# Reordering GpSimd's queue and the weight steps in the attention rounds of a decay attention, SwiGLU and maxout kernel

## The chip, the cores and the metric

One core of a Trainium2 chip runs the whole program. The metric is the device time of one execution in microseconds (us), read as the median of several. The engines are TensorE (PE; PEld is its weight load), VectorE (DVE), ScalarE (ACT), GpSimd (POOL) and SyncE (SP, which here only issues DMAs).

## The reference

A causal linear attention with a decay per head (2 x 8 heads, 768 tokens, 64 per head, blocks of 64), then an RMS norm and a SwiGLU layer (1536 tokens, 512 to 1536 to 512), then the maximum of three products and an output product (512 to 768 to 512).

```python
intra = einsum('bhic,bhjc->bhij', qb, kb) * Dmask       # Dmask = lam ** (i - j), i >= j
intra = einsum('bhij,bhjd->bhid', intra, vb)
inter = einsum('bhid,bhde->bhie', qb * lam_pow, kv_state)
out = intra + inter
kv_state = lam_block * kv_state + einsum('bhsd,bhse->bhde', kb * rev_pow, vb)
...
xn = x / sqrt(mean(x * x) + 1e-06) * rms_g
g = xn @ w_gate
x = (g * sigmoid(g) * (xn @ w_val)) @ w_out
...
h = maximum(maximum(x @ w1, x @ w2), x @ w3)
out = h @ w_out2
```

## The kernel before

Products in fp32 are made of three matmuls of halves: each operand is split into a high half (`xh`, `wh`, `hh`, a cast on ACT) and a low half (`xl`, `wl`, `hl`, the remainder, mostly on POOL).

**Attention** goes over 12 chunks of 128 tokens in software-pipelined rounds 0, 1, 2 and so on. A round is a list of steps, one letter each (`named`, L429), each of them a stage of another chunk:

- M (L379, chunk s-2): the mix of state and scores on PE into `px`, then ACT writes the squares `sq` and the scaled `x`; from chunk 4 on DVE sums the squares (`ss`, L392).
- C (L313, chunk s-1): scores and new states on PE into `sc`, from `kT`, `qT`, the scaled keys `kd` and `vn`.
- a, b (L328, chunk s-1): DVE masks the two halves into `A` (L331); a also advances the state `S` (L349). V (L353, chunk s-1) advances it once more.
- T (L288, chunk s): loads of chunk s+2 on SP, transposes of k and q on PE into `pk`, `pq`, copies `kT`, `qT` on ACT (L299, L301), `qs` on DVE (L304), and the keys scaled on POOL (`kd`, L285) for this chunk and the next, so in effect for chunk s+1.
- U (L396, chunk s-2): sum over features on PE (`pm`), `ms` on DVE (L403), and the token scale `ri`, a power, on POOL (L405).
- N (L408, chunk s-3): `pb` on PE spreads `ri` over the partitions (L414), DVE multiplies `x` by it (L416), ACT makes `xh` (L418). R (L421, chunk s-3): the low half `xl` (L427), on POOL for the first eight chunks.

All engines execute in the order in which the program issues. In rounds 0 to 6 that is M C a N b R T U V. These seven rounds run as a prologue; later rounds are mixed into the first stage, a few steps at each `gap()` (L439).

**Weights** come as 512 KB loads (L157) into three raw buffers and are turned into halves in units. `make_unit` (L242) moves three units on: it finishes the oldest (`wh` on ACT, `wl` on POOL, L167 and L170), does the three weight steps of the next on DVE (L196, L199, L202) with an addition on POOL behind them (L204), and begins a third with two ACT operations (L238, L239). In the prologue it is called four times, after steps counted by hand (L971), and seven loads are placed in the same way (L973).

**First stage**: for each block of 512 tokens and each hidden slice, a gate product `pg` and a value product `pv` (L604), activation, split, and an output product (L617). Its first product needs `xh` and `xl` of chunks 0 to 3, so N(3) and R(3) of round 6. The rest of the program (maxout and the remaining slices, L874) isn't touched.

```python
named = dict(M=(2, mixed), N=(3, normed), C=(1, scores), a=(1, masked(0)), R=(3, rest),
             b=(1, masked(1)), U=(2, summed), V=(1, advance), T=(0, lambda c: (loads_to(c + 2), turn(c))))
attn_q = [(s_, named[ch][1], s_ - named[ch][0]) for s_ in range(NCH + 3)
          for ch in ("MCaNbRTUV" if s_ <= CPNB + 2 else "MNCRaUbVT") if 0 <= s_ - named[ch][0] < NCH]
```

Of the kernel before, what the change touches and what calls it, by code (L numbers as in the profile page):

```python
# [9 lines left out]
F32 = mybir.dt.float32  # L10
F32R = mybir.dt.float32r
AF = mybir.ActivationFunctionType
ALU = mybir.AluOpType
# [5 lines left out]
P = 128  # L19
# [7 lines left out]
def tile_decay_attention_swiglu_maxout(  # L27
# [16 lines left out]
    nc = tc.nc  # L44
    B, H, S, D = q.shape
    NT, DM = out.shape
    NP = H // 2
# [5 lines left out]
    C = P // 2  # L53
# [3 lines left out]
    CPB = S // P  # L57
    NCH = NT // P
    CPNB = NB // P
# [7 lines left out]
    att = att_ctx.enter_context(tc.tile_pool(name="att", bufs=2))  # L67
# [3 lines left out]
    def bank(name):  # L71
        return psum.tile([P, 512], F32, tag="bank", name=name)
# [9 lines left out]
    Tm = attc.tile([P, H, C], F32, name="Tm")  # L82
# [3 lines left out]
    qkv = {}  # L86
    nxt_load = [0]

    def load(c, n):
        t = ld.tile([P, H, D], F32, tag="kqv"[n], name="kqv"[n] + "n", bufs=4 if n == 2 else 3)  # L90
        b, s = divmod(c, CPB)
        nc.sync.dma_start(out=t, in_=(k, q, v)[n][b, :, s * P:(s + 1) * P, :].rearrange("h p d -> p h d"))
        qkv.setdefault(c, {})[n] = t

    def loads_to(c):
        while nxt_load[0] <= min(c, NCH):
            n = nxt_load[0]
            if n:
                load(n - 1, 2)
            if n < NCH:  # L100
                load(n, 0)
                load(n, 1)
            nxt_load[0] += 1
# [7 lines left out]
    def crosswise(t, src):  # L111
        return [(t[:, 0::2], src[:, 0::2])] + [(t[HC[m], 1::2], src[HC[1 - m], 1::2]) for m in range(2)]
# [37 lines left out]
    pos = {"load": 0, "made": 0, "raw": 0, "step": 0, "gap": 0, "quiet": False, "lag": 3, "narrow": True, "seam": False}  # L150

    def load_to(n):
        while pos["load"] < min(n, len(raw_list)):
            nm, f = raw_list[pos["load"]]
            t = wp.tile([P, KD, 2 * P], I32, tag="raw", name="wraw", bufs=3)
            for to, src in crosswise(t, source[nm](f)) if nm in "gv" else [(t, source[nm](f))]:
                nc.sync.dma_start(out=to, in_=src)  # L157
            raws[nm, f] = t
            pos["load"] += 1
# [82 lines left out]
    def make_unit():  # L242

        if stage2:
            finish_unit(*stage2.pop(0))
        if stage1:
            unit = stage1.pop(0)
            for n in range(3):
                words_of_unit(n, *unit)
            stage2.append(unit[:3])  # L250
        begin_unit()
# [27 lines left out]
    keys = {}  # L279

    def decayed_keys(c):
        if c not in keys:
            keys[c] = kd = att.tile([P, H, D], F32, tag="kd", name="kd", bufs=3)
            r = slice(0, P if c % CPB != CPB - 1 else C)
            nc.gpsimd.tensor_tensor(out=kd[r], in0=qkv[c][0][r], in1=Tm[r, :, C - 1:C].to_broadcast([r.stop, H, D]),  # L285
                                    op=ALU.mult)

    def turn(c):  # L288
        kn, qn, vn = qkv[c][0], qkv[c][1], qkv[c][2]
        pk = bank("pk")  # L290
        pq = bank("pq")
        pkv = pk.rearrange("p (a t) -> p a t", t=P)
        pqv = pq.rearrange("p (a t) -> p a t", t=P)
        for a in range(NP):
            nc.tensor.transpose(pkv[:, a, :], kn[:, 2 * a:2 * a + 2, :].rearrange("p h d -> p (h d)"), ident)
        for a in range(NP):
            nc.tensor.transpose(pqv[:, a, :], qn[:, 2 * a:2 * a + 2, :].rearrange("p h d -> p (h d)"), ident)
        kT = att.tile([P, NP, P], F32, tag="kT", name="kT")
        nc.scalar.copy(out=kT, in_=pkv)  # L299
        qT = att.tile([P, NP, P], F32, tag="qT", name="qT")  # L300
        nc.scalar.copy(out=qT, in_=pqv)  # L301
        qs = att.tile([P, NP, 2, C], F32, tag="qs", name="qs")
        h0 = 0 if c % CPB else 1
        nc.vector.tensor_tensor(  # L304
            out=qs[:, :, h0:], in0=pqv.rearrange("p a (h i) -> p a h i", h=2)[:, :, h0:],
            in1=lami.rearrange("p a (h i) -> p a h i", h=1).to_broadcast([P, NP, 2 - h0, C]), op=ALU.mult)
        for n in range(c, min(c + 2, NCH)):
            decayed_keys(n)
        kd = keys.pop(c)
        A = att.tile([P, H, C], F32, tag="A", name="A")  # L310
        st[c] = dict(kT=kT, qT=qT, qs=qs, kd=kd, vn=vn, A=A)
# [16 lines left out]
    def masked(hf):  # L328
        def piece(c):
            d = st[c]  # L330
            nc.vector.tensor_tensor(  # L331
                out=d["A"].rearrange("p (a t) i -> p t a i", t=2)[:, hf],
                in0=d["sc"][hf][:, :HF].rearrange("p (a i) -> p a i", i=C),
                in1=Tm.rearrange("p (a t) i -> p t a i", t=2)[:, hf], op=ALU.mult)
            if hf == 0:
                d["S0"] = last_state[0]
                d["S1"] = next_state(c, 0, d["S0"])
        return piece
# [40 lines left out]
    def mixed(c):  # L379
        for part in range(2):  # L380
            half_mixed(c, part)
        px = st[c]["px"]
        sq = att.tile([P, NP, P], F32, tag="sq", name="sq", bufs=1)
        x = att.tile([P, NP, P], F32, tag="x", name="x")
        for n in range(2):
            nc.scalar.activation(out=sq[:, 2 * n:2 * n + 2, :], in_=px[n][:, :2, :], func=AF.Square)
        for a in range(NP):
            nc.scalar.activation(out=x[:, a, :], in_=px[a // 2][:, a % 2, :], func=AF.Copy, scale=g_sb[:, a:a + 1])
        ss = sq
        if c >= CPNB:  # L390
            ss = att.tile([P, 1, P], F32, tag="ss", name="ss", bufs=1)
            nc.vector.tensor_reduce(out=ss[:, 0, :], in_=sq.rearrange("p a t -> p t a"),  # L392
                                    axis=mybir.AxisListType.X, op=ALU.add)
        st[c] = dict(x=x, ss=ss)
# [26 lines left out]
    def rest(c):  # L421
# [5 lines left out]
        eng.tensor_tensor(out=bl[:, :, ts], in0=x, in1=bh[:, :, ts].bitcast(F32), op=ALU.subtract)  # L427

    named = dict(M=(2, mixed), N=(3, normed), C=(1, scores), a=(1, masked(0)), R=(3, rest),  # L429
                 b=(1, masked(1)), U=(2, summed), V=(1, advance), T=(0, lambda c: (loads_to(c + 2), turn(c))))  # L430
    attn_q = [(s_, named[ch][1], s_ - named[ch][0]) for s_ in range(NCH + 3)
              for ch in ("MCaNbRTUV" if s_ <= CPNB + 2 else "MNCRaUbVT") if 0 <= s_ - named[ch][0] < NCH]
    gaps = [0, 0]

    def attn_step():
        _, fn, c = attn_q.pop(0)
        fn(c)
# [505 lines left out]
    with tc.manual_schedule():  # L943
        nc.scalar.dma_start(out=lam8, in_=lam.rearrange("(o h) -> o h", o=1).to_broadcast([P, H]))
        loads_to(0)
        for to, src in crosswise(g_sb, rms_g.rearrange("(a p) -> p a", p=P)):
            nc.scalar.dma_start(out=to, in_=src)
        make_identity(nc, ident)
        nc.vector.memset(ones, 1.0)
        nc.vector.memset(zeros, 0.0)  # L950
        nc.scalar.activation(out=mhalf, in_=zeros[:, 0:1], func=AF.Silu)
        nc.vector.memset(mhalf, -0.5)
        warm = bank("warm")
        for i in range(9):
            nc.tensor.matmul(out=warm[:, 0:P], lhsT=zeros, rhs=zeros, start=True, stop=True)
        nc.vector.tensor_tensor(out=diag, in0=ident[:, :C], in1=ident[:, C:], op=ALU.add)
        for h in range(H):
            nc.vector.tensor_tensor_scan(
                out=Tm[:, h, :], data0=lam8[:, h:h + 1].to_broadcast([P, C]), data1=diag,
                initial=0.0, op0=ALU.mult, op1=ALU.add)  # L960
        for hf in range(2):
            nc.vector.tensor_copy(out=lamh[64 * hf:64 * hf + 64, :],
                                  in_=lam8.rearrange("p (a t) -> p t a", t=2)[64 * hf:64 * hf + 64, hf, :])
        for a in range(NP):
            nc.vector.tensor_tensor_scan(
                out=lami[:, a, :], data0=lamh[:, a:a + 1].to_broadcast([P, C]), data1=zeros[:, :C],
                initial=1.0, op0=ALU.mult, op1=ALU.add)
        loads_to(1)
        for i in range(sum(1 for p in attn_q if p[0] <= CPNB + 2)):
            attn_step()  # L970
            if i in (17, 26, 35, 46):  # L971
                make_unit()
            load_to(pos["load"] + (4, 8, 14, 31, 40, 48, 48).count(i))  # L973
        finish = first_stage()
        pos["step"] = len(steps)
        second_stage(finish)
# [31 lines left out]
```

## Time and profile before

| | us |
|---|---|
| median of 3 runs | 553.53 (552.24 to 554.17) |
| profiled execution | 553.25 |
| its span, first to last instruction | 551.5 |
| PE busy in the span | 531.9 (96%) |
| DVE, ACT, POOL busy | 377.5, 278.7, 316.9 |

The span is what the profile sees; 1.75 us of the execution lie around it. PE is the busy engine: from the middle of the first stage on it hardly pauses, and the first 55 us, with the attention rounds, hold most of its idle time. A row of the order of time gives start, duration, engine, line, operation, output and inputs, and in brackets the idle time before it and what released it. Starts within one engine can lie closer than the durations, since operations overlap at their ends.

### The profile page before, as it was taken

What the parts mean: (1) busy time and instruction counts of PE and PEld (TensorE: products, weight loads), DVE (VectorE), ACT (ScalarE), POOL (GpSimd) and SP (SyncE); (2) the same over time, 40 slices, a digit from 0 to 9 for tenths busy, and PEclk for the clock granted to TensorE, in tenths of its full rate; (3) what the DMA queues carried; (4) which work ended last, traced back from release to release, by engine and by line L of the source; (5) the groups of instructions that cost most, each with busy time, mean ns of one, the idle gap of its engine ahead of it and who ended that gap; (6) DMA issues with size and microseconds to landing.
All of it is one profiled execution on the core that took longest, in us unless ns stands there. A gap on an engine that the chain in (4) does not pass through costs nothing.

```text
span 551.5 us, 9707 instructions
## 1 busy us (share of the span) xinstructions
PE 531.9 (96%) x3716; PEld 440.9 (80%) x3716; DVE 377.5 (68%) x664; ACT 278.7 (51%) x541; POOL 316.9 (57%) x251
## 2 busy tenths in 40 slices
PE   7778998999999999999999999999999999999997
PEld 7776876888888888888888888888888888888885
DVE  6567988545797567566786686877777577684464
ACT  3565665354475675346346436556466655551120
POOL 2366988312799558155545737986396544962050
PEclk9876999999999999999999999999999999999999
DMA  8984566200203214121221312120123322200014
GB/s 188 228 209 121 143 160 161 64 2 1 77 0 116 76 38 116 38 71 45 78 68 47 114 40 77 40 76 13 64 78 96 97 76 76 80 35 1 0 52 178
DMA packets 65454, 44.67 MB, mean 81 GB/s; under 512 B 40064, under 2 KB 61568, under 8 KB 65408
## 3 DMA queue, kind: packets, MB, share of 16 engines
q1 hardware_dynamic: 64704, 44.05, 28.0%
q8 instruction: 29, 0.48, 0.3%
q14 instruction: 17, 0.14, 0.1%
q10 hardware_dynamic: 704, 0.01, 0.1%
HBM read 40.90 MB, written 3.15 MB: 80 GB/s over the span
## 4 chain that ended last, share of the span: by engine, by line
PE 82%; DVE 4%; POOL 4%; ACT 2%; issue 2%; DMA 1%; SPq 0%; POOLq 0%; ACTq 0%; DVEq 0%
PE p L675 34%; PE r L675 8%; PE acc L467 6%; PE acc L469 6%; PE acc L468 6%; PE q L675 4%; PE acc L858 3%; PE acc L857 3%; PE acc L859 3%; PE pv L467 2%; POOL W L204 2%; PE pv L469 1%; PE pv L468 1%; PE pg L467 1%; PE pg L469 1%
## 5 line engine op out<-in xcount | busy, mean ns | idle before, releaser
L204 POOL TENSOR_TENSOR W<-W,wraw 128x512 int32<-128x512 int32 x60 | 81.6, 1361 | 84.7 <-DVE W L202 71.6
L170 POOL TENSOR_TENSOR wl<-W,wh 128x512 fp32r<-128x512 f32 x77 | 105.3, 1368 | 42.3 <-ACT wh L167 42.1
L167 ACT CAST wh<-W 128x512 fp32r<-128x512 f32 x77 | 47.8, 620 | 87.5 <-POOL W L204 87.0
L481 POOL TENSOR_TENSOR hl<-sg,hh 128x512 fp32r<-128x512 f32 x36 | 48.7, 1352 | 25.2 <-ACT hh L480 25.2
L675 PE MATMUL p<-xh,wh 128*128 128x512 f32 x148 | 57.6, 389 | 0.0
L675 PE MATMUL p<-xl,wh 128*128 128x512 f32 x148 | 57.6, 389 | 0.0
L675 PE MATMUL p<-xh,wl 128*128 128x512 f32 x148 | 57.6, 389 | 0.0
L467 PE MATMUL acc<-hh,wh 128*128 128x512 f32 x144 | 56.6, 393 | 0.0
L468 PE MATMUL acc<-hl,wh 128*128 128x512 f32 x144 | 56.1, 389 | 0.0
L469 PE MATMUL acc<-hh,wl 128*128 128x512 f32 x144 | 56.0, 389 | 0.0
L830 DVE TENSOR_TENSOR acc_sb<-acc,acc_sb 128x512 f32<-128x512 f32 x46 | 31.8, 691 | 21.7 <-PE acc L469 20.6
L238 ACT ACTIVATE W<-wraw 128x512 f32<-128x512 f32 x60 | 40.1, 669 | 4.8 <-DMA wraw<-in_moe_w_dram 2.8
L239 ACT ACTIVATE wraw<-wraw 128x512 int32<-128x512 uint32 x60 | 39.9, 664 | 0.0
L480 ACT CAST hh<-sg 128x512 fp32r<-128x512 f32 x36 | 22.3, 619 | 33.5 <-DVE sg L614 24.9
L730 ACT COPY c<-p 128x512 f32<-128x512 f32 x34 | 19.9, 586 | 38.0 <-PE p L675 37.9
L481 POOL TENSOR_TENSOR hl<-m,hh 128x512 fp32r<-128x512 f32 x18 | 24.1, 1346 | 23.0 <-ACT hh L480 23.0
L675 PE MATMUL p<-yh,wh 128*128 128x512 f32 x90 | 35.0, 389 | 0.0
L675 PE MATMUL p<-yl,wh 128*128 128x512 f32 x90 | 35.0, 389 | 0.0
L675 PE MATMUL p<-yh,wl 128*128 128x512 f32 x90 | 35.0, 389 | 0.0
L196 DVE TENSOR_SCALAR mid<-W 128x512 f32<-128x512 f32 x46 | 31.5, 685 | 3.4 <-ACT W L238 3.4
L675 PEld LDWEIGHTS p<-xl,wh 128*128 128x128 f32 x148 | 27.8, 188 | 5.8
L675 PEld LDWEIGHTS p<-xh,wh 128*128 128x128 f32 x148 | 27.8, 188 | 5.8
(175 smaller groups left out, 1369.6 us busy)
## 6 DMA issues: line engine op xcount, KB each, us to landing
wraw<-in_moe_w_out_dram SPq DMA_DIRECT2D x18, 512.0 KB, 3.4
wraw<-in_moe_w_dram SPq DMA_DIRECT2D x18, 512.0 KB, 3.5
kn<-in_k_dram SPq DMA_DIRECT2D x12, 256.0 KB, 4.5
qn<-in_q_dram SPq DMA_DIRECT2D x12, 256.0 KB, 4.7
vn<-in_v_dram SPq DMA_DIRECT2D x12, 256.0 KB, 4.5
wraw<-in_moe_w_gate_dram SPq DMA_DIRECT2D x12, 256.0 KB, 3.0
wraw<-in_moe_w_gate_dram SPq DMA_DIRECT2D x24, 128.0 KB, 3.4
wraw<-in_moe_w_val_dram SPq DMA_DIRECT2D x12, 256.0 KB, 3.0
```

The source lines that it names most:

```text
L167: nc.scalar.copy(out=wh, in_=W.bitcast(F32))
L170: nc.gpsimd.tensor_tensor(out=wl, in0=W.bitcast(F32), in1=wh.bitcast(F32), op=ALU.subtract)
L196: nc.vector.tensor_scalar(out=mid[key].bitcast(F32), in0=W.bitcast(F32), scalar1=LEAST, scalar2=MOST, op0=ALU.max, op1=ALU.min)
L204: nc.gpsimd.tensor_tensor(out=W, in0=W, in1=lo, op=ALU.add)
L238: nc.scalar.activation(out=W.bitcast(F32), in_=hi.bitcast(F32), func=AF.Abs)
L239: nc.scalar.activation(out=lo, in_=lo.bitcast(U32), func=AF.Copy, scale=2.0 ** -29)
L467: nc.tensor.matmul(out=out, lhsT=wh, rhs=xh_, start=first, stop=False)
L468: nc.tensor.matmul(out=out, lhsT=wh, rhs=xl_, start=False, stop=False)
L469: nc.tensor.matmul(out=out, lhsT=wl, rhs=xh_, start=False, stop=last)
L481: nc.gpsimd.tensor_tensor(out=dst_l, in0=src, in1=dst_h.bitcast(F32), op=ALU.subtract)
L675: nc.tensor.matmul(out=ps, lhsT=w[:, ks], rhs=r[:, o + k, :], start=first and k == 0 and n == 0, stop=k == 1 and n == 2, skip_group_check= ...
L830: nc.vector.tensor_tensor(out=ps if kept else y, in0=ps, in1=y, op=ALU.add)
```

## The change

- POOL: `kd` of the next chunk becomes a step of its own, K, at the end of the round, and R stands behind U. So in rounds 0 to 6 POOL gets ri, xl, kd where it got xl, kd, ri. Rounds are now M C a N b T U R V K, and later M N C a U b V T K R.
- The four `make_unit` calls of the prologue stand at the ends of rounds 3, 4, 5 and 6; before, they stood behind b in rounds 3, 4 and 5 and behind T in round 6.
- The seven weight loads of the prologue stand at the ends of rounds 2 to 6 (1, 1, 1, 2, 2).
- `x` has three buffers instead of two.

```diff
@@ decayed_keys
     def decayed_keys(c):
-        if c not in keys:
-            keys[c] = kd = att.tile([P, H, D], F32, tag="kd", name="kd", bufs=3)
...
+        keys[c] = kd = att.tile([P, H, D], F32, tag="kd", name="kd", bufs=3)
...
@@ turn
-        for n in range(c, min(c + 2, NCH)):
-            decayed_keys(n)
+        if c == 0:
+            decayed_keys(0)
@@ mixed
-        x = att.tile([P, NP, P], F32, tag="x", name="x")
+        x = att.tile([P, NP, P], F32, tag="x", name="x", bufs=3)
@@ named, attn_q
-                 b=(1, masked(1)), U=(2, summed), V=(1, advance), T=(0, lambda c: (loads_to(c + 2), turn(c))))
+                 b=(1, masked(1)), U=(2, summed), V=(1, advance), T=(0, lambda c: (loads_to(c + 2), turn(c))), K=(-1, decayed_keys))
...
-              for ch in ("MCaNbRTUV" if s_ <= CPNB + 2 else "MNCRaUbVT") if 0 <= s_ - named[ch][0] < NCH]
+              for ch in ("MCaNbTURVK" if s_ <= CPNB + 2 else "MNCaUbVTKR") if (ch == "K") <= s_ - named[ch][0] < NCH]
@@ the prologue
-        for i in range(sum(1 for p in attn_q if p[0] <= CPNB + 2)):
-            attn_step()
-            if i in (17, 26, 35, 46):
+        for s_ in range(CPNB + 3):
+            while attn_q[0][0] == s_:
+                attn_step()
+            load_to(pos["load"] + (0, 0, 1, 1, 1, 2, 2)[s_])
+            if s_ > 2:
                 make_unit()
-            load_to(pos["load"] + (4, 8, 14, 31, 40, 48, 48).count(i))
```

DVE in rounds 4 and 5, before: from the state update of round 4's V over round 5 to that of round 5. W is the weight unit, sc0 and sc1 the scores of one chunk.

```order
L349 SCALAR_TENSOR_TENSOR S_615<-S_563,lami_81,sc1_529 128x64 x4
L331 TENSOR_TENSOR A_605<-sc0_667,Tm_80 128x4x64
L349 SCALAR_TENSOR_TENSOR S_702<-S_615,lami_81,sc0_667 128x64 x4
L416 TENSOR_TENSOR x_521<-x_521,pb_707 128x512
L331 TENSOR_TENSOR A_605<-sc1_668,Tm_80 128x4x64
L196 TENSOR_SCALAR W_577<-W_577 128x512
L199 TENSOR_SCALAR W_577<-W_577 128x512
L202 SCALAR_TENSOR_TENSOR W_577<-wraw_306,W_577 128x512
L304 TENSOR_TENSOR qs_744<-pq_731,lami_81 128x512
L403 TENSOR_SCALAR ms_754<-pm_749 128x1
L349 SCALAR_TENSOR_TENSOR S_758<-S_702,lami_81,sc1_668 128x64 x4
```

The same place of the changed kernel, from round 5's first mask to round 6's.

```order
L330 TENSOR_TENSOR A_593<-sc0_663,Tm_80 128x4x64
L348 SCALAR_TENSOR_TENSOR S_698<-S_604,lami_81,sc0_663 128x64 x4
L415 TENSOR_TENSOR x_519<-x_519,pb_703 128x512
L330 TENSOR_TENSOR A_593<-sc1_664,Tm_80 128x4x64
L303 TENSOR_TENSOR qs_728<-pq_715,lami_81 128x512
L402 TENSOR_SCALAR ms_736<-pm_731 128x1
L348 SCALAR_TENSOR_TENSOR S_741<-S_698,lami_81,sc1_664 128x64 x4
L196 TENSOR_SCALAR W_617<-W_617 128x512
L199 TENSOR_SCALAR W_617<-W_617 128x512
L202 SCALAR_TENSOR_TENSOR W_617<-wraw_476,W_617 128x512
L391 TENSOR_REDUCE ss_810<-sq_802 128x128
L330 TENSOR_TENSOR A_730<-sc0_812,Tm_80 128x4x64
```

The three weight steps moved from between the second mask and `qs` to behind the round's last state update and ahead of the next round's `ss` and first mask.

POOL in rounds 5 and 6, before; xl_436 from x_521 is chunk 2's low half, from x_656 chunk 3's.

```order
L170 TENSOR_TENSOR wl_713<-W_442,wh_712 128x512
L204 TENSOR_TENSOR W_577<-W_577,wraw_306 128x512
L427 TENSOR_TENSOR xl_436<-x_521,xh_435 128x4x128
L285 TENSOR_TENSOR kd_746<-kn_583,Tm_80 128x512
L405 TENSOR_TENSOR ri_756<-ms_754,mhalf_79 128x1
L427 TENSOR_TENSOR xl_436<-x_656,xh_435 128x4x128
L285 TENSOR_TENSOR kd_872<-kn_726,Tm_80 128x512
L170 TENSOR_TENSOR wl_876<-W_577,wh_875 128x512
L204 TENSOR_TENSOR W_720<-W_720,wraw_427 128x512
L405 TENSOR_TENSOR ri_890<-ms_888,mhalf_79 128x1
```

And in the changed kernel.

```order
L404 TENSOR_TENSOR ri_738<-ms_736,mhalf_79 128x1
L426 TENSOR_TENSOR xl_430<-x_519,xh_429 128x4x128
L284 TENSOR_TENSOR kd_746<-kn_573,Tm_80 128x512
L170 TENSOR_TENSOR wl_757<-W_480,wh_756 128x512
L204 TENSOR_TENSOR W_617<-W_617,wraw_476 128x512
L404 TENSOR_TENSOR ri_876<-ms_874,mhalf_79 128x1
L426 TENSOR_TENSOR xl_430<-x_656,xh_429 128x4x128
L284 TENSOR_TENSOR kd_879<-kn_710,Tm_80 128x512
L170 TENSOR_TENSOR wl_888<-W_617,wh_887 128x512
L204 TENSOR_TENSOR W_764<-W_764,wraw_611 128x512
```

Each `ri` moved ahead of the same round's `xl` and `kd`, and the weight unit's `wl` and `W` from the round's middle to its end. In round 6, chunk 3's `xl` now stands behind `ri` of chunk 4.

## Rows read from the trace of the kernel before

**Rows 1.** Busy time by stretch: first pieces of the first stage, then the rest of the interleaving.

```profile
43.50:54.00 10.50, 8.79 (x86) 5.98 (x90) 8.05 (x11) 6.04 (x15) 8.55 (x7) 0.51 0.45 115
...
55.00:120.00 65.00, 60.72 (x844) 49.14 (x841) 48.55 (x103) 36.76 (x83) 43.23 (x35) 1.00 0.44 113
```

**Rows 2.** Groups by line, 20 to 58 us: busy, mean ns, idle before and its releasers.

```profile
L414 PE MATMUL pb<-ident,ri 128*128 128x128 f32 x8 | 2.6, 422 | 4.3 <-POOL ri L405 3.5 <-DMA wraw<-in_moe_w_val_dram 0.8
...
L405 POOL TENSOR_TENSOR ri<-ms,mhalf 128x1 f32<-128x1 f32 x4 | 2.4, 592 | 0.0
...
L403 DVE TENSOR_SCALAR ms<-pm 128x1 f32<-128x1 f32 x5 | 0.7, 148 | 0.0
```

**Rows 3.** Order of time on ACT, round 3: start us, us, what.

```profile
20.36 0.62 ACT L418 CAST xh<-x 128x512 fp32r<-128x512 f32 x1 [2.41 <-DVE x L416]
...
20.89 0.67 ACT L238 ACTIVATE W<-wraw 128x512 f32<-128x512 f32 x1
...
22.03 0.56 ACT L299 COPY kT<-pk 128x512 f32<-128x512 f32 x1
```

**Rows 4.** Order of time on DVE, rounds 3 and 4.

```profile
18.49 0.42 DVE L331 TENSOR_TENSOR A<-sc,Tm 128x256 f32<-128x256 f32 x1 [2.25 <-PE sc L324]
...
19.60 0.68 DVE L416 TENSOR_TENSOR x<-x,pb 128x512 f32<-128x512 f32 x1
...
23.11 0.69 DVE L304 TENSOR_TENSOR qs<-pq,lami 128x512 f32<-128x512 f32 x1 [2.50 <-ACT qT L301]
...
23.78 0.85 DVE L349 SCALAR_TENSOR_TENSOR S<-S,lami,sc 128x64 f32<-128x64 f32 x4
...
25.11 0.42 DVE L331 TENSOR_TENSOR A<-sc,Tm 128x256 f32<-128x256 f32 x1 [0.48 <-PE sc L324]
```

**Rows 5.** Order of time on DVE, round 4: first and third weight step, POOL idle.

```profile
27.36 0.42 DVE L196 TENSOR_SCALAR W<-W 128x512 f32<-128x512 f32 x1
...
28.27 0.69 DVE L202 SCALAR_TENSOR_TENSOR W<-wraw,W 128x512 int32<-128x512 int32 x1
```

**Rows 6.** Order of time on DVE and POOL, round 6 and after: weight steps beside POOL.

```profile
44.47 0.42 DVE L304 TENSOR_TENSOR qs<-pq,lami 128x256 f32<-128x256 f32 x1 [1.32 <-ACT qT L301]
...
44.77 1.06 POOL L285 TENSOR_TENSOR kd<-kn,Tm 128x512 f32<-128x512 f32 x1
...
44.81 1.31 DVE L196 TENSOR_SCALAR W<-W 128x512 f32<-128x512 f32 x1
...
46.15 1.39 DVE L199 TENSOR_SCALAR W<-W 128x512 int32<-128x512 int32 x1
...
47.57 0.69 DVE L202 SCALAR_TENSOR_TENSOR W<-wraw,W 128x512 int32<-128x512 int32 x1
...
54.68 1.74 DVE L202 SCALAR_TENSOR_TENSOR W<-wraw,W 128x512 int32<-128x512 int32 x1
```

**Rows 7.** Order of time on DVE and POOL, round 6: ss(4), x(3), xl(3).

```profile
40.06 1.05 DVE L392 TENSOR_REDUCE ss<-sq 128x128 f32<-128x512 f32 x1 [0.79 <-ACT sq L386]
...
42.13 0.68 DVE L416 TENSOR_TENSOR x<-x,pb 128x512 f32<-128x512 f32 x1
...
43.54 1.27 POOL L427 TENSOR_TENSOR xl<-x,xh 128x512 fp32r<-128x512 f32 x1 [2.10 <-ACT xh L418]
```

**Rows 8.** Order of time on PE, first projection: the second matmul, and pb(4).

```profile
44.86 0.79 PE L468 MATMUL pg<-xl,wh 128*128 128x512 f32 x1 [0.70 <-POOL xl L427]
...
50.55 0.80 PE L414 MATMUL pb<-ident,ri 128*128 128x128 f32 x2 [0.89 <-POOL ri L405]
```

**Rows 9.** SP's queue in order of time, and time to landing of the gate loads.

```profile
18.41 0.59 SPq L92 DMA_DIRECT2D vn<-in_v_dram  x1
...
19.73 2.15 SPq L92 DMA_DIRECT2D qn<-in_q_dram  x1
...
wraw<-in_moe_w_gate_dram SPq DMA_DIRECT2D x3, 256.0 KB, 5.3
```

**Rows 10.** Order of time on PE, 94 us.

```profile
94.15 0.47 PE L467 MATMUL pv<-xh,wh 128*128 128x512 f32 x1 [1.50 <-DVE x L416]
```

More of the change, by code (lines that the diff above doesn't have):

```diff
@@ L281, in decayed_keys @@
     def decayed_keys(c):
-        if c not in keys:
-            keys[c] = kd = att.tile([P, H, D], F32, tag="kd", name="kd", bufs=3)
-            r = slice(0, P if c % CPB != CPB - 1 else C)
-            nc.gpsimd.tensor_tensor(out=kd[r], in0=qkv[c][0][r], in1=Tm[r, :, C - 1:C].to_broadcast([r.stop, H, D]),
-                                    op=ALU.mult)
+        keys[c] = kd = att.tile([P, H, D], F32, tag="kd", name="kd", bufs=3)
+        r = slice(0, P if c % CPB != CPB - 1 else C)
+        nc.gpsimd.tensor_tensor(out=kd[r], in0=qkv[c][0][r], in1=Tm[r, :, C - 1:C].to_broadcast([r.stop, H, D]),
+                                op=ALU.mult)
     def turn(c):
```

## The prediction

> **What bounds the kernel now.** I read the views in this order. The busy table by stretch: from 55 to 120 us TensorE (PE) works 60.72 of 65.00 us at full clock, and in 43.5 to 54.0, the first gated projections, it runs at a granted clock of 0.51 and is busy 8.79 of 10.50 us [rows 1]. So what a change to the attention rounds can move lies before about 55 us, plus the 4.28 us that PE idles in 55 to 120. Then the groups by line in 20 to 58 us: PE stood 4.3 us in front of `pb`, mostly waiting for GpSimd's power `ri` [rows 2]. That is the wait at which the new queue order aims. Then the order of time on VectorE (DVE), ScalarE (ACT), GpSimd (POOL) and PE in rounds 3 to 7, from which the sum is made. Rounds are counted from 0; x(3) means chunk 3's `x`. The profiled execution took 553.25 us, the median of the runs shown is 553.53; the sum goes by the former and 0.3% of it, about what a measurement can tell from no change, is 1.66 us.
>
> **Step 1, round 3: a gain of 1.6 us.** Before, ACT runs xh(0) at 20.36, then the first weight unit's two operations from 20.89, and only at 22.03 the copies kT(3) and qT(3) [rows 3]. Now the copies come first, so kT(3) starts at 20.89, 1.14 us earlier, and qs(3) on DVE at 21.97 instead of 23.11 [rows 4]. Its `ms` and the state update follow and end 24.63 - 23.11 = 1.52 us after qs starts, so at 23.49. PE's sc(3), which waited for qT(3), starts at about 22.0 and is done before that, so A(3) starts at 23.5 instead of 25.11 [rows 4]: 1.6 us ahead.
>
> **Step 2, a DVE round without weight steps: 5.0 us.** From A to x 19.60 - 18.49 = 1.11 [rows 4]. From x to qs: x lasts 0.68 with 0.08 until ACT's xh at 20.36; 0.53 until ACT's next operation (20.36 to 20.89), which is now kT; and 1.08 from kT's start at 22.03 over qT to qs at 23.11 [rows 3, 4]: 2.37. From qs to the end of S 1.52. Sum 5.0 us. pb no longer holds it up, because `ri` now stands first.
>
> **Step 3, the weight steps on DVE: 3.45 and 4.5 us, and they lie in the chain.** Alone, the three (L196, L199, L202) take from 27.36 to 28.96, 1.6 us [rows 5]. Beside a working POOL they wait: L196 beside `kd` 1.31 us instead of 0.42, L199 1.39, and the three end at 48.26 after a start at 44.81, so 3.45 us; L202 met by a POOL operation took 1.74 instead of 0.69 [rows 5, 6]. Before, rounds 4 and 5 have them after the second A and ahead of qs, where DVE waits for qT anyway and POOL stood empty. Now they come after S, while POOL goes through ri, xl and kd, all released by the `ms` just ahead, so L196 meets xl and L199 meets kd, and nothing can keep them apart. In round 4 POOL has nothing more until L202 is done: 3.45. In round 5 wl waits there as well: 3.45 + 1.74 - 0.69 = 4.5. DVE's next A is queued behind them. ACT's part of the weight steps (unit after qT) is hidden by that same DVE stretch.
>
> The Trainium skill's page SBUF — State Buffer, section Who interferes with whom, says that VectorE and GpSimd share one port pair, that whichever starts first keeps it for its whole instruction, and that `tensor_scalar` in its two-port mode and operations with two SBUF inputs fall under it. This speaks against the change, and the rows agree (1.31 against 0.42 us). By the rule the sum is the one below, +2.6; were there no such lock, it would be -2.2.
>
> **The chain.** A(3) 23.5; A(4) = 23.5 + 5.0 + 3.45 = 31.95; the sum ss(4) = 31.95 + 5.0 + 4.5 = 41.45 against 40.06; x(3), 2.07 behind it, 43.5 against 42.13 [rows 7]: **+1.4 us**, the lead of step 1 lost and more.
>
> **Step 4, the low half xl(3): +2.1 us.** The first projection's second matmul (L468, at 44.86) reads xl(3) [rows 8]. Before, xl(3) starts 43.54 - 42.13 = 1.41 after x(3) [rows 7]. Now POOL takes ri(4) ahead of it, and that needs qs(6) and ms(4): 2.37 + 0.42 + 0.15 + 0.59 = 3.53 [rows 2, 6]. That is 2.1 more, straight on PE's path, since PE is in order and nothing else stands ahead of L468.
>
> **Step 5, pb(4): -0.9 us.** PE waited 0.89 for ri(4) between two pieces of that projection [rows 8]; ri(4) now comes before xl(3), so this is gone. The earlier pb waits of rows 2 are gone too, but DVE, not PE, sets the rounds then, so they count nothing; that is what becomes of the stall the change removes.
>
> **Edits at nothing.** The third buffer of x takes away ACT's wait for an older xl; x(c) is used a round later, so a round's slack covers it. kd moves behind xl and ri and is read a round later; without that cover it would cost its 1.06 us [rows 6]. On SP's queue seven weight loads move behind attention loads, the first behind three more (v, k, q). Those three took 3.5 us of the queue, from 18.41 to 21.88, and a gate load lands 5.3 us after its issue by the median [rows 9]; a whole round lies between a load's place and its use by ACT, so I expect no wait, or little; bounds 0 and +1.0, off DVE's chain, taken as 0. What follows in 55 to 120 is reshuffled, ten steps to a round instead of nine; the longest single PE wait there is 1.50, at 94.15 [rows 10], so bounds of -1.5 and +1.5, taken as 0 for want of a row that favours a sign. Clock: up to 54.0 it was half [rows 1]. Half over the same work again: 0. The piece from pb(4) at 50.55 to 54.0, 3.45 us [rows 8], at full rate instead: -1.7; half rate for as much work more: +1.7. I take 0, what the nearest rows show for a PE that has just been waiting.
>
> **Sum:** +1.4 + 2.1 - 0.9 = +2.6. Forecast 553.25 + 2.6 = **555.8 us**, 2.3 above the median.
>
> **Rivals.**
> *Faster: the weight steps don't collide or are covered.* Then they cost 1.6 each, 7.95 - 3.2 = 4.75 less, and the sum is -2.2: 551.1 us. For it: alone they do take 1.6 [rows 5]. Against: POOL's three operations are released by the instruction right ahead. It decides once the two groups together cost under 5.3 us.
> *Same: the clock stays up.* With the waits for ri and qT gone PE idles less, and the half-rate stretch may end earlier. From L468 at 44.86 to 54.0 it is 9.1 us with 0.9 of wait, so full rate throughout would save at most 4.1, and a clock that rises in its middle 2.1: 553.7. Against: by my chain PE waits for A(4) up to some 3 us in round 6 and again for xl(3), so it idles there more than before. The Trainium skill's TensorE: Matmul & The Clock Gate (Part 1: The HAM clock gate) says that the clock has two states, falls after idling and rises with sustained work; the trace shows both levels (0.51 and 1.00), and by that rule a prologue with fewer waits would give this rival's time.
> *Same, later absorbed.* PE is not full in 55 to 120; a start 2.6 us late could be won back from its 4.28 us of waits: 553.3. Against: those waits hang on banks and DVE, not on the clock of the start.
>
> **How the numbers follow.** Forecast case 0.47 (slower). The two rivals of no change together 0.28. The uncovered gain 0.25. Low end: 551.1 less 1.7 for the clock, 549.4. High end: 555.8 plus 1.5 for a new later wait and 1.7 for the clock, 559.0. The likeliest case alone: from the edge of no change, 555.2, to 559.0. Faster 0.25, same 0.28, slower 0.47.
>
> **What would show it.** Right: L196 and L199 of rounds 4 and 5 at 1.2 us or more, directly after S; PE free of waits for ri; the gap from xh(3) to xl(3) over 2 us; L468 2 to 4 us later than 44.86. Wrong: L196 at 0.42 there, or L468 at or before 44.86; then the first rival holds. If L468 is late and the end is not, the clock row or the waits in 55 to 120 tell which of the other two it was.

## The result, and the profile after

The changed kernel takes 561.25 us (median of 4 runs, 560.44 to 562.23) against 553.85 for the kernel before in the same comparison: ratio 1.0136, 95% interval 1.0103 to 1.0169, or 7.4 us slower. The sign of the forecast was right and the size was not: +2.6 was expected, and the range ended at 559.0. The profiled execution took 560.44, its span 558.6.

Busy time by stretch of the changed kernel, for the two stretches of [rows 1] (columns: stretch, its length, then busy us of PE, PEld, DVE, ACT, POOL, then granted clock, DMA share, GB/s):

```profile
43.50:54.00 10.50, 6.95 (x76) 5.07 (x77) 7.53 (x10) 5.21 (x11) 7.48 (x7) 0.54 0.58 148
55.00:120.00 65.00, 57.35 (x801) 43.98 (x795) 49.02 (x97) 33.57 (x74) 42.52 (x35) 0.97 0.44 115
```

PE does 1.84 us less in the first stretch than in [rows 1], and 3.37 us less in the second. So more is lost behind 55 us than ahead of it.

**The prologue went as worked out.** VectorE in the changed kernel: the weight steps of round 4, then round 6 with ss(4), x(3) and ms(4):

```profile
28.29 1.48 DVE L196 TENSOR_SCALAR W<-W 128x512 f32<-128x512 f32 x1
29.81 1.16 DVE L199 TENSOR_SCALAR W<-W 128x512 int32<-128x512 int32 x1
...
40.80 1.02 DVE L391 TENSOR_REDUCE ss<-sq 128x128 f32<-128x512 f32 x1
...
42.84 0.67 DVE L415 TENSOR_TENSOR x<-x,pb 128x512 f32<-128x512 f32 x1
...
45.56 0.15 DVE L402 TENSOR_SCALAR ms<-pm 128x1 f32<-128x1 f32 x1
```

L196 takes 1.48 us here, where it took 0.42 alone [rows 5], and L199 behind it 1.16. ss(4) at 40.80 and x(3) at 42.84 are 0.7 later than in [rows 7]. These are single executions: four other runs below (e3, e6, e8, e10) have the same first rounds, and their x(3) starts between 42.56 and 44.42.

**GpSimd's queue at the end of the prologue.** First the changed kernel, then the kernel before. L170 is the low part of a weight unit:

```profile
40.95 1.28 POOL L204 TENSOR_TENSOR W<-W,wraw 128x512 int32<-128x512 int32 x1 [0.63 <-DVE W L202]
45.79 0.75 POOL L404 TENSOR_TENSOR ri<-ms,mhalf 128x1 f32<-128x1 f32 x1 [3.56 <-DMA wraw<-in_moe_w_val_dram]
46.42 1.26 POOL L426 TENSOR_TENSOR xl<-x,xh 128x512 fp32r<-128x512 f32 x1
47.64 1.51 POOL L284 TENSOR_TENSOR kd<-kn,Tm 128x512 f32<-128x512 f32 x1
49.11 1.45 POOL L170 TENSOR_TENSOR wl<-W,wh 128x512 fp32r<-128x512 f32 x1
...
101.72 1.29 POOL L170 TENSOR_TENSOR wl<-W,wh 128x512 fp32r<-128x512 f32 x1 [0.73 <-ACT wh L167]
```

```profile
45.78 1.47 POOL L170 TENSOR_TENSOR wl<-W,wh 128x512 fp32r<-128x512 f32 x1
...
95.51 1.29 POOL L170 TENSOR_TENSOR wl<-W,wh 128x512 fp32r<-128x512 f32 x1 [0.73 <-ACT wh L167]
```

GpSimd stands idle for 3.56 us in front of ri(4). The profile names a DMA, but ri starts right behind `ms` on DVE (45.56), which is its input; this is a case where the engine named isn't the one waited for. In the queue behind ri stand not only xl(3), 2.88 us later than in [rows 7], but also kd and the weight unit's low part, the second one of the program: 49.11 instead of 45.78, **3.3 us late**. The last rows of the two fences are the twelfth low part: **6.2 us late**. So the chain of weight units, which goes through DVE, POOL, ACT and POOL again, starts late and ends later still, but not by a steady growth: the fourth low part is 1.5 us late (57.29 for 55.83), the ninth 0.9 (83.63 for 82.76), and the tenth, in the third hidden slice, 5.5 (92.42 for 86.96).

**TensorE: the late start is nearly won back, and then lost.** Order of time on PE in the changed kernel:

```profile
44.27 0.80 PE L466 MATMUL pg<-xh,wh 128*128 128x512 f32 x1 [2.01 <-ACT xh L417]
...
47.74 0.79 PE L467 MATMUL pg<-xl,wh 128*128 128x512 f32 x1 [2.67 <-POOL xl L426]
...
55.72 0.50 PE L466 MATMUL pv<-xh,wh 128*128 128x512 f32 x1
```

The second matmul is 2.88 us later than in [rows 8], the first value product only 0.76 (54.96 before). Of the 2.12 us won back, 0.89 is the wait for ri(4) of [rows 8], which is gone; most of the rest is the clock. The stretch from 53 to 54 us, before and then after:

```profile
53.00:54.00 1.00, 1.00 (x11) 0.35 (x13) 1.00 (x3) 0.28 (x2) 0.22 (x1) 0.52 0.06 25
```

```profile
53.00:54.00 1.00, 1.00 (x6) 0.87 (x5) 0.00 (x0) 1.00 (x4) 1.00 (x2) 0.88 0.79 254
```

By these means (0.52 and 0.88, between levels of 0.50 and 1.00) full rate came at about 53.96 before and 53.24 after, 0.7 us earlier, though TensorE was further behind in its work. Behind that, TensorE's waits in the changed kernel from 43 to 125 us (total, times, longest) are of a kind that the kernel before hardly has there:

```profile
PE pg L467 <- POOL xl L426: 4.0, 2, 2.7
PE pg L468 <- POOL wl L170: 2.7, 2, 2.0
PE pv L468 <- POOL wl L170: 2.2, 2, 1.2
PE pg L466 <- ACT xh L417: 2.0, 1, 2.0
```

The low parts of weights, 4.9 us in four waits, are new; before, the longest single wait from 55 us on was the 1.50 for x of [rows 10].

**Why the chain loses more on its way.** ScalarE's order in the first hidden slice, changed kernel and then before (`sg` is the silu, `hh` the high half of the hidden block):

```profile
59.46 0.59 ACT L298 COPY kT<-pk 128x512 f32<-128x512 f32 x1 [1.11 <-PE pk L294]
60.42 0.62 ACT L612 ACTIVATE sg<-pg 128x512 f32<-128x512 f32 x1
61.90 0.62 ACT L479 CAST hh<-sg 128x512 fp32r<-128x512 f32 x1 [0.85 <-DVE sg L613]
```

```profile
56.04 0.58 ACT L613 ACTIVATE sg<-pg 128x512 f32<-128x512 f32 x1
59.06 0.62 ACT L480 CAST hh<-sg 128x512 fp32r<-128x512 f32 x1 [2.43 <-DVE sg L614]
...
61.24 0.57 ACT L299 COPY kT<-pk 128x512 f32<-128x512 f32 x1
```

With R gone from its place near the front of a round and ten steps dealt out instead of nine, T falls into an earlier gap, ahead of the silu. Either alone leaves it behind the silu: ten steps with R early in e6, nine steps with R late in e15. The copies wait for transposes, the silu behind them waits too, and through hh it holds GpSimd's low half hl. In the third slice it costs most. ACT, POOL and PE of the changed kernel:

```profile
87.21 0.58 ACT L298 COPY kT<-pk 128x512 f32<-128x512 f32 x1 [2.52 <-PE pk L294]
88.55 0.59 ACT L300 COPY qT<-pq 128x512 f32<-128x512 f32 x1 [0.75 <-PE pq L296]
89.03 0.60 ACT L612 ACTIVATE sg<-pg 128x512 f32<-128x512 f32 x1
```

```profile
91.19 1.28 POOL L480 TENSOR_TENSOR hl<-sg,hh 128x512 fp32r<-128x512 f32 x1 [2.91 <-ACT hh L479]
92.42 1.74 POOL L170 TENSOR_TENSOR wl<-W,wh 128x512 fp32r<-128x512 f32 x1
```

```profile
94.21 0.50 PE L468 MATMUL pg<-xh,wl 128*128 128x512 f32 x1 [0.64 <-POOL wl L170]
```

GpSimd waits 2.91 us for hh with the next weight unit queued behind it. Before, hl ran without a wait:

```profile
85.54 1.46 POOL L481 TENSOR_TENSOR hl<-sg,hh 128x512 fp32r<-128x512 f32 x1
```

From the third gate product to the fourth it is 19.5 us now (73.33 to 92.86), 14.0 before (73.94 to 87.90).

### The profile page after: what moved, and what is told of

Same layout as the page of the kernel before. It is cut to its first block, busy times and chain, and to the rows that moved or that the text cites. A ratio compares the mean times of both kernels' runs of the same rounds, so it can differ in the third digit from the quotient of the medians.

```text
span 558.6 us, 9707 instructions
## 1 busy us (share of the span) xinstructions
PE 534.4 (96%) x3716; PEld 439.5 (79%) x3716; DVE 385.1 (69%) x664; ACT 279.0 (50%) x541; POOL 317.4 (57%) x251
## 4 chain that ended last, share of the span: by engine, by line
PE 81%; POOL 7%; DVE 4%; DMA 3%; issue 2%; ACT 1%; SPq 1%; POOLq 0%; ACTq 0%; DVEq 0%
PE p L674 33%; PE r L674 8%; PE acc L466 5%; PE acc L468 5%; PE acc L467 5%; PE q L674 4%; PE acc L857 3%; PE acc L858 3%; PE acc L856 3%; POOL W L204 2%; POOL wl L170 2%; PE pv L468 2%; PE pv L466 2%; PE pv L467 1%; PE pg L467 1%
## 5 line engine op out<-in xcount | busy, mean ns | idle before, releaser
L170 POOL TENSOR_TENSOR wl<-W,wh 128x512 fp32r<-128x512 f32 x77 | 105.5, 1370 | 40.8 <-ACT wh L167 40.8
L468 PE MATMUL acc<-hh,wl 128*128 128x512 f32 x144 | 56.1, 389 | 0.0
L196 DVE TENSOR_SCALAR mid<-W 128x512 f32<-128x512 f32 x46 | 31.5, 685 | 3.4 <-ACT W L238 3.4
L199 DVE TENSOR_SCALAR mid<-mid 128x512 int32<-128x512 int32 x46 | 31.9, 694 | 0.7
```

Of the source, the lines that this page charges most:

```text
L170: nc.gpsimd.tensor_tensor(out=wl, in0=W.bitcast(F32), in1=wh.bitcast(F32), op=ALU.subtract)
L199: nc.vector.tensor_scalar(out=mid[key], in0=mid[key], scalar1=0x07FFFFFF, scalar2=3, op0=ALU.bitwise_and, op1=ALU.logical_shift_left)
L468: nc.tensor.matmul(out=out, lhsT=wl, rhs=xh_, start=False, stop=last)
```

## The experiments

Theory: the loss comes from GpSimd's weight chain, late at the start behind ri and xl(3) and later behind the hl that T's new place holds up. Rivals: the collisions on DVE, the places of the loads, the ten steps, the late place of the low halves. Each run was compared with its own runs of the kernel before (medians 552.5 to 553.9), so rows are compared by their ratios: the shift of the end is the ratio less 1, times 553 us. "Wl 12" is the start of the twelfth low part, "pv" that of the first value product, both from one profiled execution.

| run | edit against the change | median us | ratio and interval | pv | wl 12 | shift of the end |
|---|---|---|---|---|---|---|
| before | | 553.85 | 1 | 55.0 | 95.5 | 0 |
| change | | 561.25 | 1.0136 (1.0103 to 1.0169) | 55.7 | 101.7 | 7.5 |
| e1 | prologue's units back | 563.14 | 1.0188 (1.0160 to 1.0215) | 58.1 | 104.2 | 10.4 |
| e2 | prologue's xl first | 557.32 | 1.0084 (1.0059 to 1.0109) | 52.4 | 99.1 | 4.6 |
| e3 | later order back | 556.88 | 1.0065 (1.0042 to 1.0089) | 56.5 | 99.1 | 3.6 |
| e4 | loads back | 560.91 | 1.0135 (1.0110 to 1.0160) | 56.4 | 102.4 | 7.5 |
| e5 | e2 and e3 | 553.10 | 1.0010 (0.9996 to 1.0024) | 53.1 | 95.6 | 0.6 |
| e6 | later: R early, K last | 556.85 | 1.0088 (1.0059 to 1.0117) | 55.6 | 99.4 | 4.9 |
| e8 | later: R early, T ahead of b | 562.79 | 1.0185 (1.0155 to 1.0216) | 55.9 | 103.3 | 10.2 |
| e9 | e5 and prologue's units back | 553.07 | 1.0005 (0.9991 to 1.0020) | 52.9 | 94.5 | 0.3 |
| e10 | later: K ahead of T | 558.78 | 1.0093 (1.0074 to 1.0113) | 56.4 | 100.5 | 5.1 |
| e11 | e10 and prologue's xl first | 556.07 | 1.0038 (1.0022 to 1.0054) | 51.6 | 95.9 | 2.1 |
| e12 | e9 and xl of chunks 4 to 7 on DVE | 557.07 | 1.0059 (1.0038 to 1.0081) | 54.5 | 99.5 | 3.3 |
| e15 | e5 with R late | 554.37 | 1.0019 (1.0003 to 1.0034) | 51.3 | 95.6 | 1.1 |

The end goes with wl 12 (to 2.5 us in every row) and not with pv: e2 starts its value product 2.5 us before the kernel before and ends 4.6 us behind it. Against the time of the same execution, wl 12 stands 456.2 to 459.3 us ahead of the end in all 14 rows, pv 498.3 to 505.4. That makes wl 12 a good mark of the loss; it doesn't yet show that the low parts cause it.

**e1 and e4: the prologue's weight units, and its loads, at their old places.** The diff is e1's; e4 has the loads at (5, 10, 17, 36, 46, 55, 55) and the units at (25, 35, 45, 55), the ends of the rounds.

```diff
-        for s_ in range(CPNB + 3):
-            while attn_q[0][0] == s_:
-                attn_step()
-            load_to(pos["load"] + (0, 0, 1, 1, 1, 2, 2)[s_])
-            if s_ > 2:
+        for i in range(56):
+            attn_step()
+            load_to(pos["load"] + (15, 25, 35, 45, 45, 55, 55).count(i))
+            if i in (20, 30, 40, 51):
                 make_unit()
```

> The changed kernel with the four weight units of the prologue back at their old places (behind b in rounds 3 to 5, behind T in round 6); all else as changed. Theory A (the order of rounds 7 and later costs most of the 7.4 us): L196 and L199 of rounds 4 and 5 back at 0.42 us, the first projection's L468 2 to 3 us earlier, but the end within 2 us of the changed kernel, 559 to 562. Theory B (weight units made late, so that GpSimd's low halves come too late from 57 us on): 4 us or more back, 557 or less. Theory C (the places of the loads): no change, 561.

> The changed kernel with the seven weight loads of the prologue at their old places in the order of steps. Theories A and B: within 1 us of the changed kernel, 560 to 562. Theory C (the first weights reach ScalarE too late, it waited 1.4 and 1.3 us for them): 2 us or more back, 559 or less.

Measured: e1 563.14 us, 2.9 us behind the change by the ratios, and above the ranges of all three theories; e4 560.91, the same as the change. The loads count nothing, as the prediction had it. e1 does what it was made for: the weight steps of round 4 stand clear of POOL (L196 0.41 at 28.80) and x(3) comes at 41.45, 1.4 us earlier. But GpSimd has the unit at that place too, ahead of ri(4) and xl(3):

```profile
44.41 1.33 POOL L170 TENSOR_TENSOR wl<-W,wh 128x512 fp32r<-128x512 f32 x1 [2.76 <-ACT wh L167]
46.82 1.46 POOL L204 TENSOR_TENSOR W<-W,wraw 128x512 int32<-128x512 int32 x1 [1.09 <-DVE ms L402]
48.24 0.73 POOL L404 TENSOR_TENSOR ri<-ms,mhalf 128x1 f32<-128x1 f32 x1
48.94 1.48 POOL L426 TENSOR_TENSOR xl<-x,xh 128x512 fp32r<-128x512 f32 x1
```

xl(3) is 2.5 us later than in the change, and PE waits 7.08 us for it. What was won on DVE was lost in GpSimd's queue. But the second low part, at 44.41, is 4.7 us earlier here than in the change, and the end is later: a late weight unit can't be the whole of the prologue's loss, and this run goes with xl(3). The chain of weight units is late again from the fourth low part on (58.96, in the change 57.29). On ACT its high part stands behind `sq` and xh(4), which come after TensorE's `px` and `pb`:

```profile
55.34 0.66 ACT L385 ACTIVATE sq<-px 128x256 f32<-128x256 f32 x2 [5.29 <-PE px L374]
...
58.27 0.61 ACT L167 CAST wh<-W 128x512 fp32r<-128x512 f32 x1
```

So a late TensorE makes the chain late as well. The run is a miss as a test of the collisions, since it moved GpSimd's part as well; e9 is the cleaner one.

**e2: the prologue's low halves ahead of the transposes.** `"MCaNbTURVK"` becomes `"MCaNbRTUVK"`.

> The changed kernel with R in front of T and U again in the prologue, so xl(3) is no longer behind ri(4), while kd stays last. Theory A: xl(3) starts within 0.3 us of xh(3), L468 2 us earlier, end 559 to 561. Theory B: 2 to 3 us back, 558 to 559. Theory C: 561.

Measured 557.32, 2.9 us under the change by the ratios, as theory B had it (2 to 3). GpSimd there:

```profile
43.20 1.27 POOL L426 TENSOR_TENSOR xl<-x,xh 128x512 fp32r<-128x512 f32 x1 [2.06 <-ACT xh L417]
44.70 0.75 POOL L404 TENSOR_TENSOR ri<-ms,mhalf 128x1 f32<-128x1 f32 x1 [0.23 <-DVE ms L402]
45.33 1.06 POOL L284 TENSOR_TENSOR kd<-kn,Tm 128x512 f32<-128x512 f32 x1
46.35 1.72 POOL L170 TENSOR_TENSOR wl<-W,wh 128x512 fp32r<-128x512 f32 x1
```

xl(3) runs while ri would wait anyway, ri starts earlier too, and the weight unit is 2.8 us earlier than in the change. That ri waits ahead of xl is thus worth 2.9 us at the end; the same edit gives 3.0 between e3 and e5, and 3.0 between e10 and e11. From the second to the twelfth, every low part is 2.5 to 2.8 us earlier than in the change; but the first value product is 3.3 earlier too. So these pairs don't tell whether xl(3), by way of TensorE, or the weight unit behind it carries the loss.

**e3: the later rounds as before** (nine steps, key scaling in the step of the transposes), **and e5: e2 and e3 together.**

```diff
+    def turn_and_keys(c):
+        loads_to(c + 2)
+        turn(c)
+        if c + 1 < NCH:
+            decayed_keys(c + 1)
+
+    named["t"] = (0, turn_and_keys)
...
-              for ch in ("MCaNbTURVK" if s_ <= CPNB + 2 else "MNCaUbVTKR") if (ch == "K") <= s_ - named[ch][0] < NCH]
+              for ch in ("MCaNbTURVK" if s_ <= CPNB + 2 else "MNCRaUbVt") if (ch == "K") <= s_ - named[ch][0] < NCH]
```

> The changed kernel with the order of rounds 7 and later as before (M N C R a U b V T, keys inside T, nine steps to a round). Theory A: the waits of PE for wl between 65 and 100 us mostly gone, 5 us or more back: 554 to 556.5. Theory B: at most 2 us back, 559 to 561. Theory C: 561.

> The changed kernel with both undone: R ahead of T and U in the prologue, and the order of rounds 7 and later as before. What stays of the change: ri ahead of kd, units and loads at the ends of rounds, the third buffer of x. If the two losses are independent (about 3.9 us for R, 4.3 for the late order), 553 us, and the first value product starts at about 52.5 in the trace, earlier than before's 54.96, so that the end could be up to 2.5 us under before: 550 to 553. If both undo the same loss (the low halves of the weights coming late), no better than the better of the two: 556 to 557.

Measured 556.88 and 553.10. The later order costs 3.9 us (less than theory A's 5, more than B's 2), and with both undone nothing is left (1.0010, interval 0.9996 to 1.0024). The two losses add up: 2.9 and 3.9 of 7.5. But e5's value products start 1.9 us before those of the kernel before and the end isn't earlier; its wl 12 stands at 95.6, where it stood before.

**e6 and e8: which step of the later rounds.** e6 has R back at its early place and ten steps (`"MNCRaUbVTK"`); e8 is e6 with T two steps earlier, ahead of b and V (`"MNCRaUTbVK"`).

> The changed kernel with later rounds as M N C R a U b V T K: R back at its place, K still a step of its own at the end, ten steps to a round. T(7) falls back behind the first hidden slice's silu on ScalarE. Theory D (T's two copies, ahead of that silu, hold up hh, hl and the weight halves behind them on GpSimd): most of the 4.2 us back, 556 to 558. Theory E (ten steps to a round press the rounds together): no change, 560 to 562. Theory F (xl at the end of the round, next to kd, is what costs): 556 to 558.

> The changed kernel with later rounds as M N C R a U T b V K: R at its old place, but T(7) again ahead of the silu, ten steps. Theory D: 560 to 562. Theory E: 560 to 562. Theory F: 556 to 558.

Measured 556.85 and 562.79. With R early, T stands behind the silu again in the first and third slices, and 2.7 us come back, though the steps are still ten. Two places earlier for T lose 5.4 us with R as early as in e6. That speaks for theory D, though e8 lies 0.8 above its range: by E (ten steps) e6 should have stayed at 560 or more, by F (R's late place) e8 should have come to 556 to 558. In e8's third slice, on ACT and on POOL:

```profile
88.95 0.58 ACT L298 COPY kT<-pk 128x512 f32<-128x512 f32 x1 [3.84 <-PE pk L294]
```

```profile
93.25 1.28 POOL L480 TENSOR_TENSOR hl<-sg,hh 128x512 fp32r<-128x512 f32 x1 [4.99 <-ACT hh L479]
```

The longer wait (4.99 against 2.91 in the change) goes with the larger loss.

**e9: e5 with the prologue's units at their old places**, the loop of e1.

> As e5, and the four weight units of the prologue back at their old places as well. If the collisions of the weight steps with GpSimd cost the prologue what I took (two rounds of 1.85 and 2.9 us, less the unit's two ScalarE operations now in the way, 1.1 us each): 1.5 to 2.5 us faster than e5. If the places of the units hardly matter: within 0.7 us of e5. The weight steps of rounds 4 and 5 show 0.42, 0.43 and 0.69 us in either case.

Measured 553.07, against 553.10 for e5. The weight steps of rounds 4 and 5 take 0.42, 0.43 and 0.69 us here; in e5, at their new places, up to 1.37 each. So the collisions, which were worked out rightly, are worth nothing at the end (0.05% between the two ratios, well within their intervals), as long as GpSimd's queue isn't held up.

**e10 and e11: T behind K.** K and T change places in the later rounds (`"MNCaUbVKTR"`), R stays last; e11 has the prologue of e2 as well.

> The changed kernel with one edit: in the rounds beside the hidden work, key scaling stands ahead of the transposes and not behind them (order MNCaUbVKTR), so that in two of the three rounds of that part whose transposes had slid ahead of a hidden slice's silu they fall behind it again; the low halves stay last. Theory D (the late loss is the transposes' copies ahead of the silu on ScalarE, which delays the low half of the hidden block on GpSimd): 556 to 558 us, about 4 us under the changed kernel, and slice 2 of the hidden work again some 14 us long instead of 19.6. Theory G (the late loss is that the low halves stand last in the round, wherever the transposes are): 560 to 562 us, as the changed kernel.

> The edit before, and the low halves in the first rounds back ahead of the transposes (prologue order MCaNbRTUVK); low halves in the later rounds still last. Theory D with additive losses: 552.5 to 554.5 us, as the kernel before. Theory G: 556.5 to 558 us, as the run with the low halves first and the later order of the change.

Measured 558.78 and 556.07: 2.4 us under the change, and 2.5 under e2. Both lie between the ranges of theories D and G. Two pairs of runs price the swap alike, at less than the 4 us that e10 was expected to give; it moves kd ahead of T as well as T behind the silu. The silu stands ahead again (85.43 in the third slice), and POOL doesn't wait for hh:

```profile
89.11 1.16 POOL L284 TENSOR_TENSOR kd<-kn,Tm 128x512 f32<-128x512 f32 x1
90.23 1.47 POOL L480 TENSOR_TENSOR hl<-sg,hh 128x512 fp32r<-128x512 f32 x1
91.67 1.72 POOL L170 TENSOR_TENSOR wl<-W,wh 128x512 fp32r<-128x512 f32 x1
```

but hl is only 1 us earlier than in the change (2 us, counted from the first gated matmul, which this execution had 1.0 later), and the slice is still 18.8 us long (74.33 to 93.17): ri and kd now stand ahead of hl. The expectation of 14 us is a miss.

**e12: is GpSimd alone the bound?** e9 with the low halves of chunks 4 to 7 on DVE.

```diff
-        eng = nc.gpsimd if c < 2 * CPNB else nc.vector
+        eng = nc.gpsimd if c < CPNB else nc.vector
```

> The run with both orders and the weight units back at their old places, and in addition the low halves of chunks 4 to 7 on VectorE instead of GpSimd (four 128x4x128 subtractions of about 2.5 us leave GpSimd's queue). Theory H (from 47 to 108 us GpSimd's chain of weight units sets the end): 549 to 552 us, faster than before by 1 to 4 us. Rival (VectorE, which makes the second half of the weight splits and the attention's masks, is as close to full there, or GpSimd's queue has slack): 552.5 to 556 us.

Measured 557.07, 3.0 us slower than e9 by the ratios and 3.3 slower than the kernel before, where theory H had 1 to 4 faster; even the rival's range ends 1 us below it. GpSimd has four operations less (they took it 1.3 to 1.5 us each in the kernel before, not 2.5), but DVE is as full, and the weight steps and the attention's state stand in its queue. Its stretch from 65 to 75 us, and TensorE's longest wait from 43 to 100 us:

```profile
65.00:75.00 10.00, 7.56 (x52) 5.79 (x44) 9.86 (x20) 6.30 (x14) 8.04 (x7) 1.00 0.69 184
```

```profile
PE px L374 <- DVE S L348: 2.4, 1, 2.4
```

DVE is busy 9.86 of 10 us where e9 has 8.15, and TensorE waits 2.4 us for the state where e9 has 1.2. So there is no room to move this work from GpSimd to DVE. What a relief of GpSimd alone would give, the run doesn't show: that the chain of weight units through both engines paces this part is argued from the waits and from wl 12, not tested by itself.

**e15: R's place alone.** e5 with `"MNCaUbVRt"` for the later rounds.

> The run with both orders back (low halves first in the first rounds; the later rounds as before in nine steps with key scaling in the transposes' step), and one edit: in the later rounds the low halves stand behind the state's step and just ahead of the transposes (MNCaUbVRt). TensorE, ScalarE, VectorE and SyncE keep their rows, only GpSimd's queue changes. Theory I (what the swap of transposes and key scaling does not give back, some 1.4 us, is the late place of the low halves, which leave an idle gap of GpSimd at 54 us and stand ahead of a weight unit or a hidden block's low half later): 554 to 555 us. Rival (the rest is the tenth step, that is how the steps fall into the gaps): 552.5 to 553.5 us, as the run without this edit.

Measured 554.37, inside theory I's range; but by the ratios it is 0.5 us above e5, within what the two intervals allow, so theory I isn't shown. It is 1.1 us below e11, with intervals that overlap too. The expectation said that only GpSimd's queue changes; that was wrong, since taking R out moves the steps behind it one place, and some rows of PE and DVE move with them. The late place of the low halves costs little or nothing. What the swap of e11 didn't give back against e5, 1.5 us, thus seems to lie mostly in the tenth step and in kd's place; no run tells these two apart.

## Why the prediction was wrong

- **Step 1, Step 2 and The chain: right in the main, in part by luck.** A(4) came at 31.61 where 31.95 was worked out, ss(4) 40.80 for 41.45, x(3) 42.84 for 43.5. But A(3) was 0.7 us early (22.79 for 23.5) and the round behind it 0.5 longer (5.5 for 5.0), and these two cancel. The chain's +1.4 came as +0.7 in this execution, which its spread between runs (x(3) from 42.56 to 44.42) doesn't tell apart.
- **Step 3: right in the rows, without weight at the end.** L196 and L199 met POOL as said (1.48 and 1.16). By the lock of the Trainium skill's SBUF — State Buffer (Who interferes with whom) this is what happens, and the trace agrees. But e9 against e5 shows that, with xl ahead of ri, the end doesn't depend on it; in the change's own order no run has tried it alone.
- **Step 4: right for TensorE; what it left out isn't priced.** xl(3) was expected 2.1 us further behind x(3) and came 2.2 further (3.58 against 1.41), the second matmul was 2.88 late. The step followed xl(3) to TensorE, "since PE is in order and nothing else stands ahead of L468", and didn't ask what stands *behind* it in GpSimd's own queue: kd and the weight unit, 3.3 us late. Among the edits at nothing kd was called covered by a round; the weight unit behind it wasn't named. Which of the two routes carries the 2.9 to 3.0 us that this place of ri costs stays open; e1 speaks for xl(3).
- **Step 5: right**, the wait for ri(4) is gone.
- **The first rounds together: right within the spread.** e3 keeps all of the change's first rounds and undoes the later order: it is 3.6 us slower than the kernel before (interval 2.3 to 4.9), and the sum had +2.6 for these steps.
- **Third buffer, loads: taken as 0.** e4 shows it for the loads. The third buffer wasn't tried alone.
- **Clock: taken as 0, and by estimate it gave about 1 us** (most of the 1.23 won back beside the wait for ri). The second rival's mechanism (a full rate that comes earlier) did happen, together with the gone wait, and left pv only 0.76 us late. Its time, 553.7, didn't come: the loss lay behind pv.
- **The sentence that failed:** "What follows in 55 to 120 is reshuffled, ten steps to a round instead of nine; ... so bounds of -1.5 and +1.5, taken as 0 for want of a row that favours a sign." It bounded the effect of a new order by the longest wait that the old order had. The runs show in its place 3.9 us for the later order (change against e3), of which the swap that puts T behind the silu again gives back 2.4 to 2.5 (e10, e11). The changed kernel's order on ACT has kT ahead of `sg` in two hidden slices of that stretch, where the kernel before has it behind.
- **What bounds the kernel: half right.** TensorE is busy in 55 to 120, and so it seemed that only its start and its few waits could count. The chain of weight units was as close to full (POOL 9.63, 9.18 and 8.56 of 10 us in the three stretches from 55 to 85 of the kernel before), and in e2 against the change its 2.6 us at wl 12 come out as 2.9 at the end, while leads of TensorE at pv against the kernel before (1.9 to 3.6 us in e5, e9, e11 and e15) give no earlier end. The two aren't independent: by way of ACT a late TensorE delays the chain (e1).
- **The sum in other terms:** 2.9 to 3.0 for ri waiting ahead of xl and the weight unit, 2.4 to 2.5 for T's place ahead of K and the silu, about 1.5 for the rest of the later order, and 0.6 or nothing for all else, together 7.5. The rest of 1.5 is not settled further.
- **The rivals:** "later absorbed" is refuted, the loss grew instead. "Don't collide or are covered" needed 551.1; e9, with no collisions in rounds 4 and 5, gives 553.07, no gain.

No version that was run beats the kernel before: e5 and e9 equal it.

## What to carry to other kernels

When an operation is put ahead of another on an engine that works in order, follow everything that stands behind it, most of all the engine's steady production line (here the weight units), and not only the one reader that waits first. When a list of steps that is dealt out into gaps becomes one longer or loses one from its front, write out the new order of every engine around those gaps: a step that slides ahead of a producer on ScalarE costs by the wait it brings along, and the waits of the old order say nothing on that. Here a lead of the busiest engine at the start (1.9 to 3.6 us in four runs) was worth nothing at the end, with another chain as close to full.

## What the runs showed of the hardware

A short stop of TensorE can cost twice. In the changed kernel it waited 2.04 us for a low part up to 76.11, and the granted clock fell 1 us later, while it worked again:

```profile
74.00:76.00 2.00, 0.07 (x1) 0.00 (x0) 2.00 (x6) 1.35 (x3) 2.00 (x2) 1.00 0.69 215
76.00:78.00 2.00, 1.89 (x29) 1.37 (x32) 1.97 (x3) 0.65 (x2) 2.00 (x3) 0.78 0.09 20
78.00:80.00 2.00, 1.89 (x52) 1.59 (x47) 1.97 (x2) 1.38 (x3) 2.00 (x3) 0.50 0.56 143
```

Half rate (1.2 GHz, 0.50 of full) from about 77.1 to 80.5 us with TensorE busy 1.89 of 2 us means some 3 us of work that would have taken about half of that, so by estimate 1.5 us more. The kernel before has no wait over 1.50 us from 55 to 120 us, and its clock stands at 1.00 there [rows 1, 10]. In e12 the stop of 2.4 us is followed by a mean of 0.66 between 75 and 85 us.

But the length of the stop doesn't decide it. In e6 TensorE waited longer for the same low part, and the clock stayed up:

```profile
76.61 0.50 PE L468 MATMUL pg<-xh,wl 128*128 128x512 f32 x1 [2.54 <-POOL wl L170]
```

```profile
77.00:78.00 1.00, 1.00 (x20) 0.59 (x22) 1.00 (x1) 0.00 (x0) 1.00 (x2) 1.00 0.07 16
78.00:79.00 1.00, 0.89 (x61) 0.76 (x52) 0.97 (x2) 0.97 (x2) 1.00 (x1) 1.00 0.00 0
```

In e5 a stop of only 1.26 us, up to 72.54, was followed by half rate from about 74.3 to 77.7. So the same wait may cost its own length in one run and more in another. The Trainium skill's TensorE: Matmul & The Clock Gate (Part 1: The HAM clock gate) has the gate fall after idling; the changed kernel, e5 and e12 agree, where it fell behind one wait in a stretch that was busy otherwise, and e6 doesn't show it behind a longer one.
